# T5-bias attention with a leaky-ReLU feed-forward: another plan for the feed-forward pieces between the attention pairs

## The chip, the cores and the metric

The kernel runs on one core of one Trainium2 chip, in one launch. The metric is the device time of the whole execution in microseconds, the median of several runs; before the change it is 394.74 us (three runs, 394.33 to 396.08). A profile of one further execution goes with it. In profiles, PE is the matrix engine, PEld its weight loads, DVE the vector engine, ACT the scalar engine, POOL the general-purpose engine and SP the engine that here only issues transfers.

## The reference

```python
# q, k, v: (B=8, H=8, S=576, D=64);  bias_table: (32, 8)
scores = q @ k.T / sqrt(D) + bias_table[bucket(|i - j|)]   # per head
attn = softmax(scores)
x = (attn @ v)  ->  (B*S, H*D) = (4608, 512)
h = x @ w_in                      # 512 -> 2048
g = maximum(0.01 * h, h)
out = g @ w_out                   # 2048 -> 512
```

## The kernel before

**Pairs.** The attention is cut into 32 items, one for each batch and pair of heads: four pairs to a batch (`n_pairs` = 4), numbered n = 0 to 31 over all batches. For a pair, scores are made transposed (keys on the partitions). `qk_mm(n, u)` makes score chunk u on PE: u = 0 to 3 are 128 keys each for both heads (two banks of the pool `ps_s`, which has two such double banks), u = 4 are the last 64 queries against those keys (in the two single banks o0 and o1 of `ps_o`), u = 5 are the last 64 keys. `exp` turns each chunk into weights on ACT, `band` multiplies the chunk's diagonal band by the exponentiated bias on DVE. One pass later, `av_tails` and `av(n, 0)`, `av(n, 1)` multiply the weights with v on PE, in o0 and o1, and DVE divides by the row sums (`rcp`, `opair`, lines 383 and 384). o0 and o1 therefore go from `av` to chunk 4 of the next pair, which waits for both `opair`.

**How rows get turned.** From pair 7 on q and k are brought into place by a copy on DVE (`pair_rows`, line 268, one copy for q and one for k) and then a transposing transfer issued by SP (`turn_by_dma`, tile `tu`, line 276). `transpose_q` and `transpose_k` (lines 298 and 302) are the DVE copies that read `tu` one pass before it is needed. From pair 4 to pair 30 the attention output is turned by a transfer as well (`x_transposes`, `xT` <- `opair`, line 395); the last pair's is turned on PE and copied by DVE (lines 402 and 403). q, k and v come in through POOL's queue, batch by batch, in `loads(n)`; each group of loads begins with a tiny copy `tick` that waits for the output of pair n - 2.

**Feed-forward pieces.** The 4608 tokens are nine tiles T of 512. An *in-piece* (`ffn_in`, line 425) is four 128x512 matmuls over the four `xT` tiles, one for each pair of a batch in that order, into one bank; `leaky` then writes it to `gt`, on ACT (line 436), or on DVE in two steps (lines 433 and 434) for one piece in a block. There are 16 of them to a tile. An *out-piece* (`ffn_out`, line 450) is four matmuls as well; four of them, an *out-group*, add up in one bank, which is copied to `y` after the fourth (line 467 on DVE, or line 464 on ACT when `how["scalar"]` is set) and stored by SP. Sixteen out-pieces make a tile. All pieces during the attention take their banks in turn from `ps_m`, which has two; `moe_rest`, at the end, takes them from six places in turn (`bank`, line 409). `gt` has two buffers, so the in-pieces of a tile can begin only when the tile two before is wholly out (`can`).

**Passes.** The loop of line 700 runs passes n = 5 to 32. The order of a pass is written out by hand, and PE, DVE, ACT and SP each take their instructions in that order: `begin(n)` (loads, and `pair_rows` with `turn_by_dma` of a later pair m, three passes ahead, but two for m up to 9); chunks 0 and 1; `av_tails` and `av(n-1, 0)`; a first `slot()`; `av(n-1, 1)`; a second `slot()`; chunks 2, 3 and 4; `x_transposes(n-1)`; then `moe_block` with chunk 5 inside it. Before pass 5 the passes 0 to 4 are written out separately. The pass of n = 32 has no scores of its own; after it `moe_rest` does what is left.

`plan(n)` sets how many pieces the pass does (`groups_of`: all ready pieces but 4, spread evenly over the passes to the end of the batch, at least 4 and at most 8), and in which form. In a *lead* pass the two slots take two out-pieces each, with the copy to `y` on ACT; in any other pass a slot takes one in-piece. A batch's last `xT` counts as ready in pass 4k + 1 (`finished(n - 2)`). The rule `fresh` makes that pass a lead pass, so that the new tile's in-pieces come in the block, behind chunks 2 to 4. The pieces by pass before the change, in + out, follow from the rules:

```
pass     5   6   7   8   9  10  11  12  13  14  15  16  17  18  19  20
before  5+0 5+0 0+4 0+8 4+4 8+0 4+4 0+8 4+4 8+0 4+4 0+8 4+4 8+0 4+4 0+8
pass    21  22  23  24  25  26  27  28  29  30  31  32  rest
before  4+4 8+0 4+4 0+8 4+4 8+0 4+4 0+8 4+4 8+0 4+4 4+4 28+40
```

In the passes 9, 13, 17, ... the four out-pieces are in the slots and the four in-pieces in the block; in 11, 15, ... it is the other way round, with two of the four in-pieces in the slots.

Of the kernel before, what the change touches and what calls it, by code (L numbers as in the profile page):

```python
# [37 lines left out]
def kernel(  # L38
# [380 lines left out]
    def ffn_in(T, f):  # L419
        if f == 0:  # L420
            gts[T] = gt_pool.tile([P, n_fc, TT], BF16, name="gt")
        t0 = T * TT
        pm = bank("pm1")
        for c in range(n_cc):
            nc.tensor.matmul(pm, lhsT=w_in_sb[:, c, f * P : (f + 1) * P], rhs=xT[c][:, t0 : t0 + TT],  # L425
                             start=(c == 0), stop=(c == n_cc - 1))
        return pm

    def leaky(T, f, pm, by_vector=False):
        g = gts[T][:, f, :]  # L430
        if by_vector:
            low = low_pool.tile([P, TT], BF16, name="low")
            nc.vector.tensor_scalar(low, pm, 0.01, None, op0=ALU.mult)  # L433
            nc.vector.tensor_tensor(out=g, in0=low, in1=pm, op=ALU.max)  # L434
        else:
            nc.scalar.activation(g, pm, AF.Prelu, bias=0.0, scale=1.0, alpha=0.01)  # L436
# [41 lines left out]
    def can(kind):  # L478
        T = made[kind]
        if at_piece[kind]:  # L480
            return True
        if kind == "in":
            return T < made["ready"] and T < made["out"] + 2
        return T < made["in"]

    def step(kind):
        T, s = made[kind], at_piece[kind]
        at_piece[kind] = (s + 1) % n_fc
        if at_piece[kind] == 0:
            made[kind] += 1  # L490
        return T, s
# [22 lines left out]
    def groups_of(n):  # L514

        have = n_fc * (2 * made["ready"] - made["in"] - made["out"]) - at_piece["in"] - at_piece["out"]
        more = N + 1 if n > N - n_pairs else n - (n - 1) % n_pairs + n_pairs
        return max(4, min(8, (have - 4) // (more - n)))

    room = {"left": 0, "lead": False, "keep": 0}  # L520

    def plan(n):
        g = room["left"] = groups_of(n)
        fresh = n > n_pairs + 1 and n % n_pairs == 1
        room["lead"] = can("out") and g >= 8 and (fresh or not can("in"))
        room["keep"] = 4 if can("out") and not room["lead"] else 0

    def slot():
# [10 lines left out]
    def moe_block():  # L539

        done = 0
        if room["lead"] and can("in") or not can("out"):
            while done < 4 and room["left"] > 0 and can("in") and (room["lead"] or not can("out")):
                T, s = step("in")
                pm = ffn_in(T, s)
                leaky(T, s, pm, done == 1)
                room["left"] -= 1
                done += 1
                if done < 3:
                    yield  # L550
            if done < 1:
                yield
        if done < 3 and room["left"] >= 4 and can("out"):
            for part in range(4):
                piece_out()
                room["left"] -= 1
                if part == 1:
                    yield
        else:
            yield  # L560
        moe(2)
        yield
# [54 lines left out]
    def begin(n):  # L617
        loads(n)
        if n_pairs < n + 1 < N and not by_dma(n + 1):
            pair_rows(n + 1)  # L620
        for m in range(n + 2, min(n + AHEAD + 1, N)):
            if by_dma(m) and m - (AHEAD if m > 2 * n_pairs + 1 else 2) == n:
                pair_rows(m)
                turn_by_dma(m)

# [74 lines left out]
    for n in range(n_pairs + 1, N + 1):  # L700
        live = n < N
        more = n + 1 < N
        if x_by_dma(n - 2):
            finished(n - 2)
        plan(n)
        if live:
            begin(n)
            ps_a, ps_b = qk_mm(n, 0), qk_mm(n, 1)
            exp(n, 0, ps_a)
            exp(n, 1, ps_b)  # L710
        av_tails(n - 1)
        av(n - 1, 0)
        if live:
            band(n, 0)
        if more:
            transpose_q(n + 1)
        slot()
        av(n - 1, 1)
        if live:
            band(n, 1)  # L720
        if more:
            transpose_k(n + 1)
        slot()
        if live:
            ps_a, ps_b, ps_c = qk_mm(n, 2), qk_mm(n, 3), qk_mm(n, 4)
            exp(n, 2, ps_a)
        x_transposes(n - 1)
        while stores:
            o, y = stores.pop(0)
            nc.sync.dma_start(out=o, in_=y)  # L730
        if live:
            band(n, 2)
            exp(n, 3, ps_b)
        if not x_by_dma(n - 1):
            finished(n - 1)
        block = moe_block()
        if not can("out") or room["lead"] and can("in"):
            next(block)
        if live:
            exp(n, 4, ps_c)  # L740
        next(block)
        if live:
            band(n, 4)
            ps_a = qk_mm(n, 5)
            exp(n, 5, ps_a)
            band(n, 5)
        for _ in block:
            pass
    moe_rest()
# [30 lines left out]
```

## Time and profile before

| what | value |
|---|---|
| median of three runs | 394.74 us (394.33 to 396.08) |
| the profiled execution's own time | 395.22 us |
| its span, first to last instruction | 393.2 us |
| DVE busy | 214.4 us (55%) |
| ACT busy | 238.2 us (61%) |
| POOL busy | 76.6 us (19%) |
| mean granted clock of PE | 0.991 |
| PE matmuls of in-pieces, line 425 | 132.6 us busy |
| PE matmuls of out-pieces, line 450 | 132.4 us busy |

How to read it: an engine's busy time is the sum of its instructions' recorded durations, and a matmul's duration holds its way through the array, so back-to-back matmuls overlap in the record: they start about 0.216 us apart, while one takes about 0.38 us. A view of the span by windows gives, for each stretch, its length, then each engine's busy time with the number of its instructions, the share of the clock granted to PE, the load on the transfer engines (over 1 when requests of several queues are open at once) and the rate. A timeline row is: start, length, engine and line, the operation with its tiles, how many equal instructions are merged in the row, and in brackets the idle time before it with what ended it. A few matmul records are missing, so counts can be one or two short.

### The profile page before, as it was taken

How to read it: one execution, taken by the hardware profiler on the slowest of the kernel's cores; microseconds unless marked ns; L12 is line 12 of the kernel's file. 1: busy time of each engine (PE TensorE's matmuls, PEld its weight loads, DVE VectorE, ACT ScalarE, POOL GpSimd, SP SyncE). 2: the span in 40 equal slices, each digit the busy share in tenths (PEclk: the TensorE clock that was granted, in tenths of full speed). 3: DMA queues.
4: the chain of work that ended last, by engine and by line, in shares of the span. 5: the costliest groups of instructions: out<-in, count | busy, mean ns of one | idle time of the engine just before them, and what ended most of it. 6: DMA issues, size and time to landing. Idle time of an engine off the chain costs nothing.

```text
span 393.2 us, 8405 instructions
## 1 busy us (share of the span) xinstructions
PE 367.1 (93%) x3401; PEld 186.7 (47%) x3462; DVE 214.4 (55%) x536; ACT 238.2 (61%) x372; POOL 76.6 (19%) x118
## 2 busy tenths in 40 slices
PE   8778995999999999999999999999999998999995
PEld 3455543454455444544455445545454454444442
DVE  5698576566666656666667765675656442100221
ACT  4998784258855786568656874588358832466000
POOL 8764321221112220233022302210000000000000
PEclk9999998899999999999999999999999999999999
DMA  9999999999939981998399846992221010100122
GB/s 107 181 206 184 183 195 134 156 171 140 115 67 167 130 115 31 163 141 134 31 143 172 91 72 110 151 111 49 63 68 49 12 45 27 54 2 0 54 81 80
DMA packets 108734, 41.12 MB, mean 105 GB/s; under 512 B 87568, under 2 KB 103192, under 8 KB 108696
## 3 DMA queue, kind: packets, MB, share of 16 engines
q0 software_dynamic: 53696, 18.36, 44.6%
q1 hardware_dynamic: 54856, 22.10, 32.6%
q8 instruction: 27, 0.44, 0.5%
q10 hardware_dynamic: 144, 0.13, 0.1%
q14 instruction: 11, 0.09, 0.1%
HBM read 37.68 MB, written 9.45 MB: 120 GB/s over the span
## 4 chain that ended last, share of the span: by engine, by line
PE 64%; DVE 9%; ACT 6%; issue 3%; DVEq 0%; ACTq 0%
PE pm L450 30%; PE pm L425 20%; PE ps_o L380 8%; PE ps_s L320 5%; ACT at L333 4%; DVE opair L384 2%; ACT gt L436 2%; DVE at L356 2%; DVE kt L302 1%; DVE low L433 1%; DVE gt L434 1%; PE ps_o L369 1%; DVE qt L298 1%; DVE rcp L383 1%; PE ps_q L313 0%
## 5 line engine op out<-in xcount | busy, mean ns | idle before, releaser
L333 ACT ACTIVATE at<-ps_s 128x1024 bf16<-128x1024 f32 x128 | 124.0, 1030 | 26.1 <-PE ps_s L320 25.9
L425 PE MATMUL pm<-xT,w_in_sb 128*128 128x512 bf16 x546 | 132.6, 379 | 6.5 <-ACT gt L436 4.3
L450 PE MATMUL pm<-w_out_sb,gt 128*128 128x512 bf16 x546 | 132.4, 384 | 3.3 <-ACT gt L436 1.6
L436 ACT ACTIVATE gt<-pm 128x512 bf16<-128x512 f32 x123 | 74.1, 603 | 40.0 <-PE pm L425 39.7
L356 DVE TENSOR_TENSOR at<-at,hk 128x768 bf16<-128x768 bf16 (+3 forms) x160 | 69.8, 452 | 29.9 <-ACT at L333 19.2
L450 PEld LDWEIGHTS <-gt 128*128 128x128 bf16 x576 | 54.1, 99 | 63.1 <-issue 5.2
L425 PEld LDWEIGHTS <-w_in_sb 128*128 128x128 bf16 x576 | 52.6, 97 | 63.5 <-issue 9.3
L467 DVE COPY y<-pm 128x512 f32<-128x512 f32 x22 | 15.2, 692 | 69.3 <-PE pm L450 69.3
L380 PE MATMUL ps_o<-vn,at 128*128 128x65 bf16 x1280 | 49.4, 194 | 0.7
L380 PEld LDWEIGHTS <-at 128*128 128x128 bf16 x1280 | 44.4, 98 | 8.8 <-issue 0.7
L320 PE MATMUL ps_s<-qt,kt 64*128 64x512 bf16 x256 | 39.9, 381 | 1.7 <-ACT at L333 1.0
L383 DVE RECIPROCAL rcp<-ps_o 128x5 f32<-128x5 f32 x64 | 12.4, 194 | 48.2 <-PE ps_o L380 48.2
L464 ACT COPY y<-pm 128x512 f32<-128x512 f32 x13 | 7.6, 585 | 46.1 <-PE pm L450 46.1
L606 POOL COPY tick<-opair 1x1 bf16<-1x1 bf16 x18 | 4.6, 255 | 158.0 <-DVE opair L384 158.0
L384 DVE TENSOR_TENSOR opair<-ps_o,rcp 128x320 bf16<-128x320 f32 x64 | 31.5, 492 | 3.6 <-DVE rcp L383 0.4
L340 ACT ACTIVATE at<-ps_s 128x576 bf16<-128x576 f32 x32 | 22.4, 700 | 3.6 <-PE ps_s L324 3.6
L336 ACT ACTIVATE at<-ps_q 128x256 bf16<-128x256 f32 x64 | 22.0, 416 | 3.3 <-PE ps_q L313 3.2
L120 POOL DMA_DIRECT2D vn<-in_v_dram x24 | 21.6, 905 | 6.7 <-PE ps_s L320 2.3
L320 PEld LDWEIGHTS <-kt 64*128 64x128 bf16 x256 | 8.3, 94 | 27.2 <-issue 25.9
L433 DVE TENSOR_SCALAR low<-pm 128x512 bf16<-128x512 f32 x21 | 14.5, 691 | 9.8 <-PE pm L425 9.8
L459 ACT COPY y<-pm 128x256 f32<-128x256 f32 x1 | 0.4, 372 | 27.5 <-DVE y L458 27.5
L302 DVE COPY kt<-tu 128x576 bf16<-128x576 bf16 x25 | 17.0, 678 | 0.0
(57 smaller groups left out, 218.9 us busy)
## 6 DMA issues: line engine op xcount, KB each, us to landing
out_dram<-y SPq DMA_DIRECT2D x35, 256.0 KB, 2.8
qn<-in_q_dram POOLq DMA_DIRECT2D x14, 288.0 KB, 6.2
kn<-in_k_dram POOLq DMA_DIRECT2D x14, 288.0 KB, 7.3
vn<-in_v_dram POOLq DMA_DIRECT2D x28, 128.0 KB, 7.3
w_in_sb<-in_moe_w_in_dram POOLq DMA_DIRECT2D x2, 1024.0 KB, 12.9
w_out_sb<-in_moe_w_out_dram POOLq DMA_DIRECT2D x2, 1024.0 KB, 18.0
qn<-in_q_dram POOLq DMA_DIRECT2D x4, 144.0 KB, 3.9
kn<-in_k_dram POOLq DMA_DIRECT2D x4, 144.0 KB, 4.1
```

Of the source, the lines that this page charges most:

```text
L120: nc.gpsimd.dma_start(out=vn[i][:, c, :, 0:D], in_=v[b, :, c * P : (c + 1) * P, :].rearrange("h s d -> s h d"),)
L302: nc.vector.tensor_copy(out=kt[:, 0:S].rearrange("p (r c) -> p r c", c=NC), in_=turned_pair(n, 1))
L320: nc.tensor.matmul(ps[:, e, :], lhsT=kt[r, u * P : (u + 1) * P], rhs=qt[r, 0:512], start=True, stop=True)
L333: nc.scalar.activation(at[:, :, u, 0:512], ps, AF.Exp, scale=scale)
L336: nc.scalar.activation(at[:, e, :, 512:S], ps[e][:, 0 : NJ * SL].rearrange("p (c i) -> p c i", i=SL), AF.Exp, scale=scale)
L340: nc.scalar.activation(at4[:, 0:S], ps.rearrange("p e i -> p (e i)")[:, 0:S], AF.Exp, scale=scale)
L356: nc.vector.tensor_tensor(out=o, in0=o, in1=m, op=ALU.mult)
L380: nc.tensor.matmul(ps[:, ic, :], lhsT=at[:, o : o + P], rhs=vn[b % NBUF][:, c, 2 * p + e, :], start=False, stop=(ic == NJ and c == NJ - 1))
L384: nc.vector.tensor_tensor(out=opair[:, :, e * D : (e + 1) * D], in0=ps[:, :, 0:D], in1=rcp.to_broadcast([P, NJ + 1, D]), op=ALU.mult)
L425: nc.tensor.matmul(pm, lhsT=w_in_sb[:, c, f * P : (f + 1) * P], rhs=xT[c][:, t0 : t0 + TT], start=(c == 0), stop=(c == n_cc - 1))
L436: nc.scalar.activation(g, pm, AF.Prelu, bias=0.0, scale=1.0, alpha=0.01)
L450: nc.tensor.matmul(pm, lhsT=gt[:, f, ts * P : (ts + 1) * P], rhs=w_out_sb[:, f, :], start=(f == 0), stop=(f == n_fc - 1))
```

## The change

```diff
@@ groups_of
-        return max(4, min(8, (have - 4) // (more - n)))
+        keep = min(n_fc, 4 * ((n - 1) // n_pairs)) if more <= N else 0
+        return max(4, min(8, (have - keep) // (more - n)))
@@ plan
-        fresh = n > n_pairs + 1 and n % n_pairs == 1
-        room["lead"] = can("out") and g >= 8 and (fresh or not can("in"))
+        room["lead"] = can("out") and g >= 8 and not can("in")
@@ moe_block
-        if room["lead"] and can("in") or not can("out"):
-            while done < 4 and room["left"] > 0 and can("in") and (room["lead"] or not can("out")):
-                T, s = step("in")
-                pm = ffn_in(T, s)
-                leaky(T, s, pm, done == 1)
-                room["left"] -= 1
-                done += 1
-                if done < 3:
-                    yield
-            if done < 1:
+        while not can("out") and can("in") and done < 4 and room["left"] > 0:
+            T, f = step("in")
+            leaky(T, f, ffn_in(T, f), done == 1)
+            room["left"] -= 1
+            done += 1
+            if done < 3:
                 yield
-        if done < 3 and room["left"] >= 4 and can("out"):
+        while done < 2:
+            done += 1
+            yield
+        if can("out") and room["left"] >= 4:
@@ begin
-            if by_dma(m) and m - (AHEAD if m > 2 * n_pairs + 1 else 2) == n:
+            if by_dma(m) and m - (AHEAD if m > 2 * n_pairs + 2 else 2) == n:
@@ the passes from 5 on
-        if live:
-            band(n, 2)
-            exp(n, 3, ps_b)
-        if not x_by_dma(n - 1):
+        if not live:
             finished(n - 1)
+            break
+        band(n, 2)
         block = moe_block()
-        if not can("out") or room["lead"] and can("in"):
+        next(block)
+        exp(n, 3, ps_b)
+        next(block)
+        exp(n, 4, ps_c)
+        if can("out"):
             next(block)
-        if live:
-            exp(n, 4, ps_c)
-        next(block)
-        if live:
-            band(n, 4)
-            ps_a = qk_mm(n, 5)
-            exp(n, 5, ps_a)
-            band(n, 5)
+        band(n, 4)
+        ps_a = qk_mm(n, 5)
+        exp(n, 5, ps_a)
+        band(n, 5)
         for _ in block:
             pass
```

What it does: the number of pieces that `groups_of` holds back grows by 4 with each batch up to 16, in place of a constant 4. A pass is a lead pass only when no in-piece can be done. So from pass 21 on every pass has the same shape: one in-piece in each slot, one whole out-group around chunk 5 in the block, and two in-pieces after it. In a block without out-pieces the first in-piece and its `leaky` now stand before `exp` of chunk 3. The rows of pair 10 are copied and turned in pass 8, next to those of pair 11, and no longer in pass 7. In pass 32 nothing follows the last pair's turn, so the pieces after it belong to `moe_rest` with its six places. By the rules:

```
pass     5   6   7   8   9  10  11  12  13  14  15  16  17  18  19  20
after   5+0 5+0 0+4 0+8 3+4 7+0 6+0 0+8 3+4 3+4 7+0 3+4 3+4 3+4 3+4 7+0
pass    21  22  23  24  25  26  27  28  29  30  31  32  rest
after   4+4 4+4 4+4 4+4 4+4 4+4 4+4 4+4 4+4 4+4 4+4 2+0 34+52
```

The pieces are the same 144 + 144 in all. The pieces whose `leaky` runs on DVE go from 21 to 6, the full copies to `y` on ACT (line 464) from 13 to 2. In the passes 9, 13, 17, 21, 25 and 29 the new tile's first in-piece stands in the first slot, directly behind `av(n-1, 0)`.

## The prediction

> **What bounds the kernel now.** I read the page first: busy shares, the slices, the chain of waits.
>
> ```profile
> span 393.2 us, 8405 instructions
> ...
> PE 367.1 (93%) x3401; PEld 186.7 (47%) x3462; DVE 214.4 (55%) x536; ACT 238.2 (61%) x372; POOL 76.6 (19%) x118
> ...
> DMA  9999999999939981998399846992221010100122
> ...
> PE 64%; DVE 9%; ACT 6%; issue 3%; DVEq 0%; ACTq 0%
> ```
>
> PE is busy for 93% of the span and makes up 64% of the chain that ended last; no other engine reaches 10% of it. The transfer engines are full for eleven slices of 9.8 us, then with a nearly idle slice in every four. So two questions matter: where PE still waits, and whether an early wait is really one for transfers.
>
> Next the view by windows, cut where `av_tails` starts on PE: the passes 7, 9, 21, 22, 23 and 24, then all from pass 32 on.
>
> ```profile
> 58.97:73.19 14.22, 9.67 (x85) 4.55 (x84) 6.58 (x19) 5.35 (x9) 1.50 (x3) 0.76 1.74 138
> 83.12:93.61 10.49, 10.11 (x100) 5.14 (x100) 7.73 (x19) 6.88 (x11) 2.86 (x4) 1.00 1.58 189
> ...
> 206.93:217.41 10.48, 10.10 (x100) 5.12 (x100) 7.71 (x19) 6.87 (x11) 2.87 (x4) 1.00 1.06 152
> 217.41:227.89 10.48, 9.98 (x100) 5.13 (x100) 6.47 (x16) 8.72 (x15) 3.11 (x5) 1.00 1.01 120
> 227.89:238.24 10.35, 9.97 (x100) 5.13 (x100) 6.29 (x15) 6.61 (x12) 0.00 (x0) 1.00 0.17 34
> 238.24:248.17 9.93, 9.82 (x100) 5.07 (x100) 6.04 (x16) 5.46 (x9) 2.62 (x4) 1.00 1.16 144
> ...
> 320.30:393.20 72.90, 67.50 (x353) 31.39 (x359) 10.55 (x18) 19.46 (x33) 0.00 (x0) 1.00 0.12 44
> ```
>
> The passes 21 to 24 hold eight pieces each and the same attention work, but take 10.48, 10.48, 10.35 and 9.93 us. The shortest has only out-pieces; the others lose 0.55, 0.55 and 0.42 us. From pass 9 to 31 the pattern repeats every four passes. The timeline of PE shows the loss, in pass 22 and then in pass 24:
>
> ```profile
> 218.28 0.81 PE L425 MATMUL pm<-xT,w_in_sb 128*128 128x512 bf16 x3
> ...
> 223.31 0.19 PE L324 MATMUL ps_s<-qt,kt 128*128 128x64 bf16 x1
> 223.78 0.81 PE L425 MATMUL pm<-xT,w_in_sb 128*128 128x512 bf16 x3 [0.27 <-ACT gt L436]
> 224.76 2.75 PE L425 MATMUL pm<-xT,w_in_sb 128*128 128x512 bf16 x12 [0.18 <-DVE gt L434]
> ...
> 245.88 0.19 PE L324 MATMUL ps_s<-qt,kt 128*128 128x64 bf16 x1
> 245.91 1.89 PE L450 MATMUL pm<-w_out_sb,gt 128*128 128x512 bf16 x8
> ```
>
> After the last matmul of chunk 5 the next piece starts 0.03 us later in pass 24, 0.47 us later in pass 22: it waits for a bank of `ps_m` that `leaky` on ACT still reads, and one piece on for the bank that DVE reads (0.11 us beyond four matmuls of 0.216). Up to chunk 5 nothing is lost: 223.31 is 5.90 us behind the pass's start with four pieces done, 245.88 is 7.64 with six, and two pieces are 1.73. So an in-piece in a slot costs PE only its matmuls; two or more in the block cost a wait.
>
> **Part by part: the passes 21 to 31.** Before, six of them lose 0.55 and three 0.42: 4.56 us. After, all are alike, with two in-pieces in the slots, an out-group around chunk 5 and two in-pieces behind. ACT is not in the way: it is busy for 8.72 us in the pass of in-pieces alone and 5.46 in the one of out-pieces, and a half-and-half pass lies between, below 9.93. The one new wait is the last in-piece's: it takes the bank of the out-group, with one in-piece between.
>
> ```profile
> 237.80 0.61 PE L320 MATMUL ps_s<-qt,kt 64*128 64x512 bf16 x4
> ...
> 237.90 0.69 DVE L467 COPY y<-pm 128x512 f32<-128x512 f32 x1 [2.15 <-PE pm L450]
> ```
>
> In pass 23 the out-group ends where the next chunk starts, at 237.80, and the copy to `y` at 238.59, 0.79 us later. The in-piece between covers 0.87, less the passing of the semaphore, so I take 0.1 us; the bounds are 0 and 0.7 (a copy wholly uncovered). Eleven times 0.1 is 1.1: **a gain of 3.5 us**, between a loss of 3.1 and a gain of 4.6.
>
> **The passes 9 to 20, banks alone.** Before: three times 1.52, 4.56 us. After: passes 12 and 8 are unchanged lead passes, seven have an out-group in the block and lose nothing (three in-pieces, so none behind a fresh out-group's bank), and four have in-pieces alone (10, 11, 15, 20) and keep a loss of 0.55, since the piece on DVE still holds its bank as long: 2.2. Moving the first `leaky` ahead of chunk 3's `exp` only shifts which of the two banks is late. **Gain 2.4 us**; bounds 0 (every moved wait comes back) and 4.6. The twelve pieces fewer before pass 32 and more behind it cost the same on PE at either place: 0.
>
> **The rows of pair 10.** The 14.22 us of pass 7, with only four pieces and the clock at 0.76, are the longest loss. PE, DVE and the transfer of pair 8's rows:
>
> ```profile
> 61.05 0.61 PE L320 MATMUL ps_s<-qt,kt 64*128 64x512 bf16 x4
> 64.33 0.20 PE L313 MATMUL ps_q<-qt,kt 64*128 64x64 bf16 x1 [2.67 <-DVE opair L384]
> 65.85 0.39 PE L313 MATMUL ps_q<-qt,kt 64*128 64x64 bf16 x7 [1.31 <-DVE opair L384]
> ...
> 63.23 0.36 DVE L268 COPY pr<-kn 96x768 bf16<-96x768 bf16 x1 [1.21 <-DMA kn<-in_k_dram]
> ...
> 64.53 0.64 DVE L298 COPY qt<-tu 128x576 bf16<-128x576 bf16 x1
> ...
> 65.30 0.49 DVE L384 TENSOR_TENSOR opair<-ps_o,rcp 128x320 bf16<-128x320 f32 x1
> ...
> L276 SPq DMA_TRANSPOSE tu<-pr x1: 1717/1717/1717, 53.1 to 53.1; - x1
> DMA to landing us min/median/max: 10.9/10.9/10.9
> ```
>
> Chunk 4 waits for `opair`, which DVE does late because pair 10's second copy waited for k until 63.23. Taking that copy away seems to free over 3 us. But DVE's next hold stands right behind it: the copy `qt` of line 298 reads pair 8's `tu`, issued at 53.1 and landed 10.9 us later, at 64.04. `qt` ran at 64.53, so everything from there moves by **0.5 us**; that landing hangs on transfers issued before the change acts. In pass 8, DVE takes pair 10's and pair 11's copies together; `av` there has two out-pieces behind it, so this hides. The bounds of the gain are 0 and the whole wait, 65.85 less 61.5, 4.4 us, if that landing did not bind.
>
> **The first in-piece of a tile.** In pass 9 the piece moves from behind chunk 4 into the first slot. Its fourth matmul needs the `xT` of pair 7. The issues on SP, the piece on PE, and three transfers of `xT` with their landings:
>
> ```profile
> 74.11 2.03 SPq L276 DMA_TRANSPOSE tu<-pr  x1
> 77.36 2.19 SPq L395 DMA_TRANSPOSE xT<-opair  x1
> ...
> 88.81 1.90 PE L425 MATMUL pm<-xT,w_in_sb 128*128 128x512 bf16 x7
> ...
> L395 SPq DMA_TRANSPOSE xT<-opair x1: 2192/2192/2192, 77.4 to 77.4; - x1
> DMA to landing us min/median/max: 9.7/9.7/9.7
> ...
> L395 SPq DMA_TRANSPOSE xT<-opair x1: 2131/2131/2131, 67.6 to 67.6; - x1
> DMA to landing us min/median/max: 12.2/12.2/12.2
> ...
> L395 SPq DMA_TRANSPOSE xT<-opair x1: 1364/1364/1364, 118.7 to 118.7; - x1
> DMA to landing us min/median/max: 6.8/6.8/6.8
> ```
>
> Before, `xT` landed at 77.4 + 9.7 = 87.1 and the piece began at 88.81: no wait. After, pass 9 starts at 83.12 - 0.5 = 82.6; the slot comes 0.87 us later (218.28 less 217.41), its fourth matmul 0.65 after that: 84.1. SP now issues two `tu` ahead of this `xT` (74.11 - 0.5 = 73.6, 2.03 each), so `xT` goes out at 77.7, not 76.9. Landing takes 6.8 us at least (the transfer issued at 118.7, in a thinner stretch) and 12.2 at most (issued at 67.6, right behind a `tu`). Its own row says 9.7, the one behind a `tu` 12.2, and it is now behind two; I take the middle, 11: 88.7, and PE waits from 84.1: **a loss of 4.6 us**, bounds 0.4 (landed at 84.5) and 5.8 (at 89.9). Queued behind it on PE are `av(8, 1)` and the chunks 2 to 5 of pair 9, so ACT and DVE idle too; no cover is left.
>
> At the later batch starts (13, 17, 21, 25) the same matmul is due 9.93 + 0.87 + 0.65 = 11.45 us after the start of the pass before, and `xT` is issued 4.17 after it (77.36 less 73.19): 7.3 us for landing, where 6.8 was seen. A shorter pass before it takes up to 0.9 off. I put 0.1 at each: **a loss of 0.4 us**, bounds 0 and a rival's price below.
>
> **The end.** PE from pass 32 on:
>
> ```profile
> 326.08 2.75 PE L425 MATMUL pm<-xT,w_in_sb 128*128 128x512 bf16 x12 [0.39 <-ACT y L464]
> 329.51 1.02 PE L425 MATMUL pm<-xT,w_in_sb 128*128 128x512 bf16 x4 [0.69 <-ACT gt L436]
> ...
> 361.45 27.79 PE L450 MATMUL pm<-w_out_sb,gt 128*128 128x512 bf16 x125
> ```
>
> The last pair's turn has nothing behind it, and PE idles 0.39 us; three in-pieces then wait for the two banks, 329.51 less (326.08 + 2.59) = 0.84, and 0.2 more before line 450 goes on. After, an out-group and two in-pieces, 5.2 us, cover the turn's copy, and `moe_rest` has six places. The four-matmul pieces there run at 27.8 us for 128 matmuls either way. I leave 0.1 for the shorter cover ahead of the turn: **gain 1.3 us**, bounds 0.5 and 1.5.
>
> **The sum**, against the profiled execution's 395.22: -0.5 + 4.6 + 0.4 - 2.4 - 3.5 - 1.3 = -2.7, so 392.5. The median lies 0.48 below that execution: **392.0 us**, 0.7% faster.
>
> **The rivals.**
>
> *The clock drops in pass 9.* A wait of 4.6 us is as long as the one of pass 7 (from 61.5 to 65.85, with one short matmul in it), and there the clock fell:
>
> ```profile
> 65.80:67.00 1.20, 0.93 (x9) 0.52 (x10) 1.17 (x4) 0.66 (x2) 0.00 (x0) 0.50 2.06 119
> ```
>
> It was granted at 0.50 behind that wait, and 0.76 over the 14.22 us is 3.4 us of clock lost, some 0.5 of it before PE had work: 2.9 us. Then 394.9. For it: the like length. Against it: most of the range of the wait is shorter. The Trainium skill (TensorE: Matmul & The Clock Gate, Part 1) says that one idle window of about 3.4 us halves the clock, and that the windows run free of the program; the row agrees that a wait beyond that length can do it, and by the rule a wait of 4.6 us need not fill a window.
>
> *No wait in pass 9.* With pair 10's rows gone from pass 7, the transfers have less ahead of them, and `xT` lands in 6.8 us, with a wait of 0.4 left: 387.8. Against it: the same transfers are only issued later, directly ahead of this one.
>
> *Slower: the batch starts wait on transfers every time.* Before, the rule `fresh` kept 5 us between a landing and its first reader. If the denser passes make `xT` land in 9.7 us at the passes 13, 17, 21 and 25, each waits 9.7 - 7.3 = 2.4 us: 392.0 - 0.4 + 9.6 = 401.2. It decides from a landing time of 7.3 us on. For it: 6.8 is only half a microsecond away, and a store of `y` now goes out ahead in nearly every pass. Against it: from slice 12 on the transfer engines have a slack slice in each batch, so loads no longer pile up from one to the next.
>
> *The change doesn't do what it says* holds for pair 10's rows, and is in the sum.
>
> **How the numbers follow.** A measurement of this kernel can tell about 0.5% from no change, 2.0 us: faster is below 392.8, slower above 396.7. The forecast has 0.45, with a range of its own of 389 to 394 (the wait of pass 9 and the copy to `y` between their bounds), two thirds of it faster: 0.30 faster, 0.15 same. The clock's drop has 0.20: 0.17 same, 0.03 slower. No wait has 0.17, faster. Waits at every batch have 0.18: 0.16 slower, 0.02 same. Together 0.47, 0.34 and 0.19. The range of 387.0 to 398.0 takes in the first two, nearly all of the third and leaves most of the fourth out.
>
> **What would show it.** In the profile after: passes 21 to 31 at 10.0 us each, with a short idle before the last in-piece that ends with DVE's `y`; pass 7 at 13.7 us, with chunk 4 still late and `qt` waiting for `tu`; in pass 9 an idle of line 425 that ends with a transfer of `xT`, and behind it the granted clock, 1.0 or 0.5; no waits around 326 us before the end's run. Wrong would make it: an idle before line 425 in every pass 4k + 1, passes with four and four pieces above 10.4 us, or pass 7 shorter by 3 us.

## The result, and the profile after

The changed kernel takes **393.35 us** (median of 13 runs, 388.46 to 399.91) against 396.08 us for the kernel before on the same chip (13 runs, 394.18 to 400.43): a ratio of 0.989, interval 0.985 to 0.993, so 1.1% faster. The ratio, like those below, sets only the runs within 1.5% of each kernel's fastest against each other (here 8 against 11); by the medians of all runs the change is 0.7%. Ten further runs of it gave 0.990 (0.985 to 0.994). Its first profiled execution, 396.43 us, was longer than that median, so a second one of 390.33 us is read beside it; the two differ most in pass 9.

The page of the first profile, as far as it answers to the lines shown of before:

```profile
span 394.6 us, 8469 instructions
...
PEclk9999999977999999999999999999999999999999
...
PE 81%; DMA 10%; DVE 5%; ACT 2%; issue 1%; POOL 0%; POOLq 0%
```

PE is still the bound. New are the 10% of the chain that is now a wait for transfers (half of it for loads of k, a quarter each for `xT` and `tu`, by the page's next row), and two slices (78.9 to 98.6 us) with the clock granted at 0.7. The view by windows says where the time went. First the first profile (passes 7, 9, 20 and 21, and everything from pass 32 on), then the second (passes 7 and 9, the passes 10 to 31 as one window, and the rest; pass 8 takes 9.93 us in all three):

```profile
59.05:68.66 9.61, 6.84 (x87) 3.66 (x85) 5.54 (x16) 5.27 (x9) 1.35 (x2) 1.00 1.80 128
...
78.59:99.31 20.72, 10.67 (x98) 5.35 (x96) 6.99 (x18) 6.38 (x10) 2.88 (x4) 0.75 1.47 121
191.59:201.22 9.63, 9.24 (x100) 4.68 (x97) 6.57 (x17) 8.13 (x14) 2.99 (x4) 1.00 1.19 152
201.22:211.23 10.01, 10.01 (x102) 5.07 (x100) 6.18 (x15) 7.04 (x12) 2.88 (x4) 1.00 1.46 108
...
310.82:394.60 83.78, 78.03 (x408) 35.99 (x407) 10.56 (x18) 22.46 (x38) 0.00 (x0) 1.00 0.12 44
```

```profile
60.70:72.01 11.31, 8.25 (x85) 4.06 (x84) 5.54 (x16) 5.26 (x9) 1.47 (x2) 0.85 1.81 138
...
81.94:92.19 10.25, 9.18 (x98) 4.68 (x96) 6.92 (x18) 6.39 (x10) 2.87 (x4) 1.00 1.39 171
92.19:304.29 212.10, 208.19 (x2118) 107.01 (x2151) 130.50 (x324) 153.46 (x240) 37.82 (x55) 1.00 0.75 102
304.29:388.50 84.21, 77.45 (x400) 35.99 (x407) 10.56 (x18) 22.46 (x38) 0.00 (x0) 0.99 0.12 44
```

Set against the windows of before, where the passes 10 to 31 take 320.30 - 93.61 = 226.69 us, and with each piece that moved (12 more from pass 32 on) priced at 27.8 / 32 = 0.87 us, the sum of the prediction reads, in us:

```
                                        predicted   first profile   second profile
start of pass 7                             0            0.1             1.7
pass 7                                     -0.5         -4.6            -2.9
pass 9, piece counted (wait 4.6 - 0.55)    +4.1        +11.1            +0.6
passes 10 to 31 (-1.85 - 3.5 + 0.4)        -5.0         -5.6            -5.0
from pass 32 to the last matmul            -1.3         -1.3            -1.5
behind the last matmul                      0           +1.8            +2.4
span against before (393.2)                -2.7         +1.4            -4.7
```

Here "passes 10 to 31" is -15.2 and -14.6 us as measured, less the eleven pieces gone from them (9.55). Pass 7 began between 58.8 and 60.7 us in the profiles of this kernel and its variants; none of that is put down to the change. The dense part came out as forecast. PE's waits for `leaky`, summed before and then after (us in total, times, longest):

```profile
PE pm L425 <- ACT gt L436: 4.3, 15, 0.7
...
PE pm L450 <- ACT gt L436: 1.6, 6, 0.3
```

```profile
PE pm L425 <- DVE gt L434: 1.6, 4, 0.4
...
PE pm L425 <- ACT gt L436: 0.2, 1, 0.2
```

The waits for ACT are gone but for 0.2 us; those for DVE's piece go from 1.1 us before to 1.6. A pass with four and four pieces takes 10.01 us (10.03 predicted), and its last in-piece's wait for the bank is the 0.07 us by which the first of these rows exceeds a pair of pieces without a wait (1.90); the second shows pass 32 going through its turn without an idle:

```profile
218.89 1.97 PE L425 MATMUL pm<-xT,w_in_sb 128*128 128x512 bf16 x8
...
314.44 3.62 PE L450 MATMUL pm<-w_out_sb,gt 128*128 128x512 bf16 x16
317.90 15.70 PE L425 MATMUL pm<-xT,w_in_sb 128*128 128x512 bf16 x72
```

The four passes with in-pieces alone keep their wait for DVE's piece, 0.4 each (the first row of after). Pass 20 takes 9.63 us for its seven pieces, where pass 14 of the second profile, with an out-group in its block, takes 9.06: 0.57 more.

**Pass 9.** First PE and SP of the first profile, then of the second, and for each the two issues of `tu` on SP (count, shortest, middle and longest in ns) and the landing of that `xT`:

```profile
79.45 0.81 PE L425 MATMUL pm<-xT,w_in_sb 128*128 128x512 bf16 x3
90.32 0.59 PE L425 MATMUL pm<-xT,w_in_sb 128*128 128x512 bf16 x1 [10.05 <-DMA xT<-opair]
...
79.98 2.38 SPq L395 DMA_TRANSPOSE xT<-opair  x1
...
L276 SPq DMA_TRANSPOSE tu<-pr x2: 3961/5110/6258, 69.6 to 73.6; - x2
...
DMA to landing us min/median/max: 10.3/10.3/10.3
```

```profile
84.64 0.38 PE L425 MATMUL pm<-xT,w_in_sb 128*128 128x512 bf16 x1 [1.01 <-DMA xT<-opair]
...
77.89 1.34 SPq L395 DMA_TRANSPOSE xT<-opair  x1
...
L276 SPq DMA_TRANSPOSE tu<-pr x2: 1339/2392/3445, 72.9 to 74.4; - x2
...
DMA to landing us min/median/max: 6.7/6.7/6.7
```

The reader is the same matmul in both, the fourth of that in-piece, but it is due at 80.1 us in one (79.45 + 3 x 0.216) and at 83.5 in the other. The two `tu` ahead of `xT` take SP 10.2 or 4.8 us, `xT` then lands after 10.3 or 6.7 us, and PE waits 10.05 or 1.01 us. The two kernels of *The end* below have the same passes 7 to 9; in their profiles `xT` landed after 6.0 and 6.9 us, and PE waited 1.3 and 1.9.

**Pass 7.** DVE's `qt` and PE's chunk 4 and first out-piece, in the first profile and then PE in the second:

```profile
62.86 0.64 DVE L298 COPY qt<-tu 128x576 bf16<-128x576 bf16 x1 [1.63 <-DMA tu<-pr]
...
64.19 0.29 PE L313 MATMUL ps_q<-qt,kt 64*128 64x64 bf16 x7 [2.63 <-DVE opair L384]
64.41 1.90 PE L450 MATMUL pm<-w_out_sb,gt 128*128 128x512 bf16 x8
```

```profile
65.91 0.31 PE L313 MATMUL ps_q<-qt,kt 64*128 64x64 bf16 x7 [2.70 <-DVE opair L384]
...
66.97 2.69 PE L450 MATMUL pm<-w_out_sb,gt 128*128 128x512 bf16 x6 [0.22 <-issue]
```

Chunk 4 still waits for `opair`, and `opair` behind `qt` for the landing of `tu`. In the first profile `qt` ran at 62.86 in place of 64.53 and PE's clock did not fall (eight matmuls in 1.90 us); in the second six matmuls take 2.69 us, the half clock. Five more profiles have the same pass 7 (pair 7 on PE, `tu` behind `xT`, pass 9 as a lead pass, and the two of *The end*): it takes 9.6, 10.9, 11.3, 11.6, 11.9, 13.3 and 13.5 us in the seven. Most of that spread is the clock. Its share over the window gives the time at half clock as length x (1 - share) / 0.5: none in the first profile, 3.3 to 3.5 us in the next four, 6.7 to 6.9 in the last two, as in pass 7 of before (14.22 x 0.24 / 0.5 = 6.8).

**The end.** The last matmuls on PE and ACT's issue of the last store, before, after (first profile), and the page's row on the fetching of ACT's instructions in both (packets, MB, share):

```profile
379.80 9.44 PE L450 MATMUL pm<-w_out_sb,gt 128*128 128x512 bf16 x42
...
390.14 0.37 ACTq L461 DMA_DIRECT2D out_dram<-y  x1
...
q14 instruction: 11, 0.09, 0.1%
```

```profile
379.62 9.23 PE L450 MATMUL pm<-w_out_sb,gt 128*128 128x512 bf16 x42
...
389.75 2.13 ACTq L461 DMA_DIRECT2D out_dram<-y  x1
...
q14 instruction: 12, 0.10, 0.1%
```

Before, the span ends 4.0 us behind the last matmul (393.2 - 389.24), after it 5.75 us (394.6 - 388.85), 6.4 in the second profile. ACT's issue takes 2.13 us in place of 0.37 (2.59 in the second profile), and one more block of instructions was fetched. That q14 is ACT's queue is inferred: its count changes when ACT's program does, while the other instruction queue, q8, shows 27 in every profile.

### The profile page after: what moved, and what is told of

Same layout as the page of the kernel before. It is cut to its first block, busy times and chain, and to the rows that moved or that the text cites. A ratio compares the mean times of both kernels' runs of the same rounds, so it can differ in the third digit from the quotient of the medians.

```text
span 394.6 us, 8469 instructions
## 1 busy us (share of the span) xinstructions
PE 365.7 (93%) x3462; PEld 184.4 (47%) x3462; DVE 203.5 (52%) x517; ACT 240.3 (61%) x376; POOL 76.7 (19%) x118
## 4 chain that ended last, share of the span: by engine, by line
PE 81%; DMA 10%; DVE 5%; ACT 2%; issue 1%; POOL 0%; POOLq 0%
PE pm L450 32%; PE pm L425 28%; PE ps_o L380 9%; PE ps_s L320 7%; DMA kn<-in_k_dram 5%; DMA xT<-opair 3%; DMA tu<-pr 3%; ACT at L333 1%; PE ps_o L369 1%; PE ps_s L323 1%; DVE opair L384 1%; PE ps_q L313 1%; DVE at L356 1%; DVE low L433 1%; DVE gt L434 1%
## 5 line engine op out<-in xcount | busy, mean ns | idle before, releaser
L425 PE MATMUL pm<-xT,w_in_sb 128*128 128x512 bf16 x576 | 140.7, 381 | 11.9 <-DMA xT<-opair 10.1
L436 ACT ACTIVATE gt<-pm 128x512 bf16<-128x512 f32 x138 | 83.0, 602 | 101.0 <-PE pm L425 100.4
L356 DVE TENSOR_TENSOR at<-at,hk 128x768 bf16<-128x768 bf16 (+3 forms) x160 | 71.4, 453 | 33.7 <-ACT at L336 18.9
L450 PEld LDWEIGHTS <-gt 128*128 128x128 bf16 x576 | 53.0, 98 | 60.6
L467 DVE COPY y<-pm 128x512 f32<-128x512 f32 x33 | 22.8, 692 | 76.5 <-PE pm L450 76.5
L380 PEld LDWEIGHTS <-at 128*128 128x128 bf16 x1280 | 44.9, 98 | 19.1 <-issue 11.3
L120 POOL DMA_DIRECT2D vn<-in_v_dram x24 | 22.9, 959 | 7.1 <-PE ps_s L324 3.7
L298 DVE COPY qt<-tu 128x576 bf16<-128x576 bf16 x25 | 16.3, 651 | 7.0 <-DMA tu<-pr 7.0
L112 POOL DMA_DIRECT2D qn<-in_q_dram x18 | 13.8, 768 | 3.7 <-DMA qn<-in_q_dram 1.5
```

The source lines that it names most:

```text
L120: nc.gpsimd.dma_start(out=vn[i][:, c, :, 0:D], in_=v[b, :, c * P : (c + 1) * P, :].rearrange("h s d -> s h d"),)
L356: nc.vector.tensor_tensor(out=o, in0=o, in1=m, op=ALU.mult)
L380: nc.tensor.matmul(ps[:, ic, :], lhsT=at[:, o : o + P], rhs=vn[b % NBUF][:, c, 2 * p + e, :], start=False, stop=(ic == NJ and c == NJ - 1))
L450: nc.tensor.matmul(pm, lhsT=gt[:, f, ts * P : (ts + 1) * P], rhs=w_out_sb[:, f, :], start=(f == 0), stop=(f == n_fc - 1))
L467: nc.vector.tensor_copy(out=y, in_=pm)
```

## The experiments

Two theories on the early passes. The *late-transfer theory*: the wait of pass 9 is one of order; `xT` of pair 7 stands on SP's queue behind two `tu`, and its reader has come forward from the block to the first slot, so that either another place for the issue or another place for the reader removes it. The *backlog theory*: the loads of the first 90 us bound these passes, and what is won at one landing is lost at the next. On the end, the *fetch theory*: ACT's instructions have grown until a new block begins right at the last store. Ratios below are to the kernel before on the same chip, with their intervals.

**The changed kernel again.** No edit.

> The changed kernel once more, as the partner of the other three. First theory (late transfer): PE waits 8 to 10 us before line 425 in pass 9 for the xT of pair 7, which SP issues only after two tu transfers whose issue took 10.3 us in the profiled run; time 0.989 of before. Rival (backlog): the same wait, but it is the sum of all transfers up to some 90 us that ends it, not the place of any one. Both expect the same here: pass 7 near 9.6 us, pass 10 starting at 96 to 99 us.

Measured: 392.49 us (389.69 to 397.05), 0.990 (0.985 to 0.994). Its profile is the second one above.

**The wait of pass 9 taken away in three ways.** Pair 7's output turned on PE in place of SP:

```diff
-        return n_pairs <= n < N - 1
+        return n_pairs <= n < N - 1 and n != 2 * n_pairs - 1
...
-        if x_by_dma(n - 2):
+        if n - 2 >= n_pairs:
```

> The output of pair 7 alone is turned on PE and copied by DVE, as the last pair's is, in place of a transfer. Late transfer: no wait for xT in pass 9; what is left is pair 10's tu, which holds qt on DVE until about 85 us and so chunk 4 until 86.5; pass 10 starts at 91 to 92 us in place of 99.3, and the time falls by 6 to 8 us against the changed kernel, to 0.970 to 0.975 of before. Backlog: the wait goes to tu and to the loads of k instead, pass 10 starts at 96 or later, and the time falls by less than 3 us.

Measured: 389.43 us, 0.981 (0.973 to 0.989). Pair 11's `tu` issued behind that `xT`, no longer ahead of it:

```diff
-                turn_by_dma(m)
+                if m != 2 * n_pairs + 3:
+                    turn_by_dma(m)
...
         x_transposes(n - 1)
+        if n == 2 * n_pairs:
+            turn_by_dma(n + AHEAD)
```

> Only the place on SP's queue changes: the turn of pair 11's rows is issued behind the xT of pair 7 in pass 8 and no longer ahead of it. Late transfer: xT goes out near 74 us and lands at 82 to 85, the wait in pass 9 falls to 2 to 5 us, the time by 5 to 7 us against the changed kernel, to 0.971 to 0.976 of before. Backlog: xT still lands at 88 or later and the time falls by less than 2 us.

Measured: 388.65 us (387.11 to 389.65), 0.979 (0.971 to 0.987). And the reader put back into the block, in pass 9 alone, as the rule `fresh` had it:

```diff
-        room["lead"] = can("out") and g >= 8 and not can("in")
+        fresh = n == 2 * n_pairs + 1
+        room["lead"] = can("out") and (fresh or g >= 8 and not can("in"))
```

> Pass 9 alone is made a lead pass as before the change: the out-group in the slots, the new tile's three in-pieces in the block. Late transfer: the xT of pair 7 lands where it did, at 84 to 90 us, but its first reader comes some 5 us later in the pass, so the wait for it shrinks by up to 5 us and the bank waits of the block (0.4 to 0.6 us) come back; pass 9 takes 9.5 to 10 us where the landing is early, 12 to 15 where it is late; time 0.981 to 0.986 of before, with less spread than the changed kernel. Backlog: pass 9's length does not depend on where the piece stands, time 0.988 to 0.992.

Measured: 387.24 us (387.09 to 387.57), 0.973 (0.965 to 0.981). The window of pass 9 with pair 7 on PE, SP's issue of `xT` and PE's first in-piece with the other order, and PE in pass 9 with the lead pass:

```profile
81.01:90.08 9.07, 8.97 (x98) 4.68 (x97) 7.05 (x18) 6.39 (x10) 2.87 (x4) 1.00 1.57 194
```

```profile
74.78 1.43 SPq L395 DMA_TRANSPOSE xT<-opair  x1
...
81.42 1.19 PE L425 MATMUL pm<-xT,w_in_sb 128*128 128x512 bf16 x4
```

```profile
87.72 1.90 PE L425 MATMUL pm<-xT,w_in_sb 128*128 128x512 bf16 x8
```

With `xT` issued at 74.78 in place of 77.9 to 80.0, the in-piece of pass 9 runs through (four matmuls in 1.19 us); with its reader at 87.72 in place of 79.5 to 82.8, nothing waits either, though `xT` goes out as late as 77.2. The wait goes when either place is changed, as the late-transfer theory has it; the backlog's signs (pass 10 at 96 or later, `xT` landed at 88 or later) did not come. The three ratios lie 0.9 to 1.7 hundredths below that of the changed kernel, the last with its whole interval below 0.985, the lower end of that kernel's; the other two intervals overlap it. The first two gain less than was expected (0.970 to 0.976), the third more (0.981 to 0.986): the expectations reckoned with the wait of the first profile, which three of the four profiles with the same passes 7 to 9 do not have. With the lead pass `xT` landed at 84.5 (77.2 + 7.3), so in that profile the reader in the slot, due at 83.55, would have waited only 1 us. About 2 us of that last one's gain come from the end, not from pass 9: there ACT's last issue takes 0.38 us and the span ends 4.1 us behind the last matmul (below); in the other two it takes 2.4 us, between the 2.13 and 2.59 of the changed kernel. All 16 runs of these three kernels and the next one lie between 385.8 and 390.9 us; the 23 of the changed kernel between 388.5 and 399.9.

**The same for all four pairs of that batch.** The outputs of the pairs 4 to 7 turned on PE, so that no `xT` stands ahead of pair 8's `tu` either:

```diff
-        return n_pairs <= n < N - 1
+        return 2 * n_pairs <= n < N - 1
...
-        if x_by_dma(n - 2):
+        if n - 2 >= n_pairs:
```

> The outputs of the pairs 4 to 7 are turned on PE and copied by DVE, so that four transposing transfers fewer stand on SP's queue in passes 5 to 8. Late transfer: the tu of pair 8 is no longer behind two xT and lands at 58 to 61 us, qt in pass 7 does not wait for it, pass 7 takes 7.5 to 8.5 us without a clock drop, and pass 9 waits for no xT; what is left is the load of k for pair 12, 0 to 3 us on DVE in pass 9; time 0.965 to 0.974 of before. Backlog: tu and the loads land no earlier, pass 10 starts at 90 or later, time above 0.978.

Measured: 388.5 us (385.82 to 390.88), 0.976 (0.964 to 0.987). The `qt` of pass 7 on DVE:

```profile
63.65 0.65 DVE L298 COPY qt<-tu 128x576 bf16<-128x576 bf16 x1 [0.98 <-DMA tu<-pr]
```

The expected earlier `tu` did not come: `qt` still waits for it until 63.65, where the profiles of the other kernels have 62.9 to 65.3. The chain of waits shows why: the load of pair 8's k ends at 53.2 after 17.2 us, `tu` goes out at 53.58 (51.7 to 54.1 in the others) and lands after 10.05 us, with no `xT` about. That landing does not hang on SP's order; here the backlog theory holds (pass 10 begins at 90.66; the ratio lies between the two expectations).

**Pair 10's rows.** The move undone in the changed kernel (the diff), and the move alone made in the kernel before (its reverse):

```diff
-            if by_dma(m) and m - (AHEAD if m > 2 * n_pairs + 2 else 2) == n:
+            if by_dma(m) and m - (AHEAD if m > 2 * n_pairs + 1 else 2) == n:
```

> Only the move of pair 10's rows is undone. Late transfer: pass 7 is back at 13 to 14.5 us with DVE held by the load of k until 63, the xT of pair 7 goes out behind one tu and lands near 87, so the wait in pass 9 shrinks to about 2.5 us; pass 10 starts at 94 to 95, 4 us earlier than the changed kernel, time 0.978 to 0.98 of before. Backlog: what pass 7 loses pass 9 gains, pass 10 starts within 1.5 us of the changed kernel's, time 0.985 to 0.993.

> The kernel before, with only the move of pair 10's rows to pass 8. If the move gains by itself: pass 7 falls from 14.2 to 9.6 to 11.5 us, and since the first in-piece of the new tile stands in the block of pass 9 the later xT costs 0 to 2 us there; time 0.990 to 0.994 of before. If it gains nothing (the prediction's sum gave it 0.5 us): 0.998 to 1.002, pass 7 at 13.5 us or longer, or the gain of pass 7 lost again in pass 9.

Measured: undone, 394.92 us (391.67 to 399.77), 0.987 (0.976 to 0.999); made alone, 394.41 us (10 runs), 0.995 (0.990 to 0.999). Undone, DVE and PE in pass 7; made alone, the same two:

```profile
63.59 0.36 DVE L268 COPY pr<-kn 96x768 bf16<-96x768 bf16 x1 [2.80 <-DMA kn<-in_k_dram]
...
66.20 0.39 PE L313 MATMUL ps_q<-qt,kt 64*128 64x64 bf16 x7 [1.31 <-DVE opair L384]
```

```profile
64.55 0.64 DVE L298 COPY qt<-tu 128x576 bf16<-128x576 bf16 x1 [2.55 <-DMA tu<-pr]
...
65.88 0.39 PE L313 MATMUL ps_q<-qt,kt 64*128 64x64 bf16 x7 [3.85 <-DVE opair L384]
```

Without the move DVE waits for k until 63.59, with it for `tu` until 64.55, and chunk 4 comes at 66.20 or 65.88. The next hold stands right behind the first, as the prediction said. Made alone, pass 7 takes 13.76 us in place of 14.22, close to the 0.5 of the prediction, and pass 10 begins 0.1 us earlier in that profile; the ratio gives about half a per cent, and no profile shows where more than 0.5 us would come from. Undone, only one `tu` stands ahead of `xT`, which goes out at 77.68, and PE still waits 1.70 us in pass 9, so the second `tu` is not needed for a wait.

**Pass 7 shortened on purpose.** Pass 7 as a lead pass, its out-pieces in the slots ahead of chunk 4; then the passes 7 and 9 both; then both with pair 11's `tu` behind `xT` of pair 7 as above:

```diff
-        room["lead"] = can("out") and g >= 8 and not can("in")
+        fresh = n == 2 * n_pairs - 1
+        room["lead"] = can("out") and (fresh or g >= 8 and not can("in"))
```

```diff
-        fresh = n == 2 * n_pairs - 1
+        fresh = n == 2 * n_pairs - 1 or n == 2 * n_pairs + 1
```

> Pass 7 alone is made a lead pass: its four out-pieces stand in the slots, ahead of the chunk 4 that waits for DVE, and no longer behind it. Late transfer, with pass 9 as in the changed kernel: PE has 3.5 us of work before the wait, so pass 7 has little idle time and no clock drop and takes 6.5 to 8 us in place of 9.6 to 13.5; but pass 9 then comes to the xT of pair 7 all the earlier, whose landing stays at 84 to 90 us, and waits 6 to 13 us; pass 10 starts at 92 to 99, the time stays at 0.982 to 0.990 of before. Rival (pass 7's wait and half clock are a loss of their own): pass 10 starts 4 to 6 us earlier, time 0.970 to 0.976.

> Passes 7 and 9 are lead passes; SP's order is the changed kernel's. Late transfer: pass 7 as in the run before, but the xT of pair 7 goes out behind two tu and lands at 82 to 89, so pass 9 waits 0 to 6 us in its block; pass 10 starts at 87 to 93, time 0.962 to 0.975 of before, with more spread than the run before. Backlog: the same as the run before within 1 us.

> Passes 7 and 9 are lead passes, and the turn of pair 11's rows is issued behind the xT of pair 7. Late transfer: pass 7 at 6.5 to 8 us without a clock drop, the xT of pair 7 out near 70 us and landed at 78 to 83, its first reader at 82 or later; pass 10 starts at 85 to 89 us, time 0.958 to 0.968 of before. Backlog: the loads and tu end pass 9 at 90 or later whatever PE does, time 0.970 to 0.976.

Measured: 394.96 us (10 runs), 0.990 (0.986 to 0.995); 391.16 us, 0.986 (0.976 to 0.995); 387.12 us (385.57 to 392.60), 0.971 (0.963 to 0.979). PE with pass 7 as a lead pass, and SP's two `tu`; PE in pass 9 with both; DVE and PE in pass 9 with the order changed as well:

```profile
65.54 0.29 PE L313 MATMUL ps_q<-qt,kt 64*128 64x64 bf16 x7 [0.33 <-DVE opair L384]
...
89.47 0.58 PE L425 MATMUL pm<-xT,w_in_sb 128*128 128x512 bf16 x1 [7.92 <-DMA xT<-opair]
...
L276 SPq DMA_TRANSPOSE tu<-pr x2: 4117/5034/5951, 69.1 to 73.3; - x2
```

```profile
89.34 2.29 PE L425 MATMUL pm<-xT,w_in_sb 128*128 128x512 bf16 x5 [3.42 <-DMA xT<-opair]
```

```profile
83.43 0.73 DVE L298 COPY qt<-tu 128x576 bf16<-128x576 bf16 x1 [2.58 <-DMA tu<-pr]
...
86.95 1.24 PE L425 MATMUL pm<-xT,w_in_sb 128*128 128x512 bf16 x5 [1.07 <-DMA xT<-opair]
```

The wait ahead of chunk 4 falls to 0.33 us, and the time of the whole does not move: the reader of `xT` comes earlier, SP's `tu` take 4.1 and 6.0 us, and 7.92 us are waited in pass 9, within the 6 to 13 that the late-transfer theory expected. With pass 9 a lead pass too, 3.42 us remain, and the time misses what either theory gave; with the order changed, 1.07, and then `qt` waits for a `tu` until 83.43. There pass 10 begins at 90.24 and the ratio is 0.971, which is what the backlog theory expected (90 or later, 0.970 to 0.976), not the late-transfer theory. In the four profiles without a long wait in pass 9 that have pair 7 on PE or the later `tu`, pass 10 begins at 89.8 to 90.7 us. So both theories have a part: the order decides who waits in pass 9, the landings how much there is to win before it. Whether another order of the loads would let pass 10 begin earlier was not tried.

**The end.** The last half store issued by SP in place of ACT, and three small copies at the kernel's start moved from ACT to DVE, so that ACT has three instructions fewer:

```diff
-            nc.scalar.dma_start(out=o[:, h:DM], in_=y[:, h:DM])
+            nc.sync.dma_start(out=o[:, h:DM], in_=y[:, h:DM])
```

```diff
-        copy = nc.scalar.copy if j % 3 == 2 else nc.vector.tensor_copy
-        copy(out=ub[:, C0 + lo : C0 + lo + m * w].rearrange("h (m w) -> h m w", w=w),
+        nc.vector.tensor_copy(out=ub[:, C0 + lo : C0 + lo + m * w].rearrange("h (m w) -> h m w", w=w),
```

> The last half row block's store is issued by SP in place of ACT; nothing else. In five profiles of kernels with the new plan that issue on ACT took 2.1 to 2.6 us, before 0.37, and the end came 6.1 to 6.3 us behind the last matmul in place of 4.1; their ACT queue shows a twelfth fetch of instructions, before eleven. Fetch theory: the issue waits for that block of instructions, so from SP it takes 0.4 us and the end comes 4.0 to 4.6 us behind the last matmul; time 2 us below the changed kernel, near 0.984 to 0.986 of before. Rival (the store itself is slow at the end): the end stays 6 us behind.

> Three small copies that build the bias row, at the start of the program, go from ACT to DVE; nothing else changes. Fetch theory: ACT's program is three instructions shorter, the twelfth fetch of its instructions goes away or moves off the last issue, that issue takes 0.4 us and the end comes 4.1 us behind the last matmul in place of 6.2; time 2 us below the changed kernel, near 0.984 of before. Rival (the last store is slow by itself): 6 us behind, time as the changed kernel.

Measured: 391.5 us (388.81 to 398.79), 0.982 (0.962 to 1.002), and 391.47 us (389.07 to 396.27), 0.981 (0.973 to 0.990). The last matmuls, the last issue (line 460 there) and the fetches with three instructions fewer on ACT:

```profile
379.78 4.91 PE L449 MATMUL pm<-w_out_sb,gt 128*128 128x512 bf16 x22
...
385.59 0.37 ACTq L460 DMA_DIRECT2D out_dram<-y  x1
...
q14 instruction: 11, 0.09, 0.1%
```

The issue is back at 0.37 us, the twelfth fetch is gone, and the span ends 4.1 us behind the last matmul (388.8 - 384.69) in place of 5.75 and 6.4. With the store on SP the twelfth fetch stays, the issue takes 0.38 us there, and the end is 4.7 us behind. (The expectation's 6.1 to 6.3 us for the end is 5.75 to 6.4 by the profiles.) Set side by side, the fourteen profiles read:

```
ACT busy instructions   372  373  376  377  376              376
fetches on q14           11   11   11   12  12, once 13       12, store on SP
profiles                  2    1    1    3   6                 1
last issue, us         0.37 0.37 0.38 0.37  2.13 to 2.59      0.38
```

The count of busy instructions alone does not tell where a block begins, since issues and semaphores are not in it. A store that is slow by itself is ruled out, since from SP its issue takes 0.38 us and the end comes sooner; that a fetch falls right into ACT's issue is inferred from these counts, as no view times the fetch. The profiles agree with the fetch theory; the medians of these two, which still have pass 9's wait, are too widely spread to price it.

## Why the prediction was right

The forecast was 392.0 us, 0.7% faster, and the median came out at 393.35 us, 2.7 us below that of the kernel before on the same chip; the ratio gives 1.1%. The dense passes came out by their mechanism. That the whole came so near is in part luck: pass 7 gained more than forecast, pass 9 lost less in three of four profiles and far more in one, and the end lost what the forecast did not have; these partly cancel. Point by point:

- **Passes 10 to 31: right, in mechanism and size.** -5.6 and -5.0 us against -5.0; passes of 10.01 us against 10.03; the all-in passes kept a loss of 0.57 (0.55 predicted), 0.4 of it the wait, the copy to `y` cost 0.07 (0.1). The 0.4 us for the later batch starts was no more than that: the second profile has such waits of 1.4 us in all, 1.0 of it in pass 9.
- **Up to the last matmul: right,** -1.3 and -1.5 against -1.3.
- **The wait for `xT` in pass 9: right in place and cause, mis-sized.** The forecast was 4.6 us, and four profiles of that pass show 1.0, 1.3, 1.9 and 10.05. Two steps were off. "I take the middle, 11" for the landing: it was 6.0, 6.7, 6.9 and 10.3. In the second profile `xT` went out at 77.89, as forecast (77.7), and the short landing alone made the short wait. And "pass 9 starts at 83.12 - 0.5 = 82.6" held the reader fixed: in the first profile pass 9 starts at 78.59, 4.0 us earlier, while `xT` landed at 90.3, only 1.6 later than the forecast's 88.7; the two are the excess. There the step "SP now issues two `tu` ahead of this `xT` (74.11 - 0.5 = 73.6, 2.03 each), so `xT` goes out at 77.7" was off as well, by 2.3 us. A transposing issue has no fixed length in this stretch. In the ten profiles that have both `tu` next to each other, ahead of or without that `xT`, the start of the first and the time that SP spent on the two were (us):

```
start  69.1  69.6  70.1  71.7  72.3  72.9  73.0  73.4  74.0  74.0
both   10.1  10.2   8.2   5.8   3.4   4.8   4.0   5.5   5.8   4.1
```

  The three that went out before 71 us took the longest; that they then stand deeper in the loads is a reading of this table, not shown by itself. The longest issues go with the earliest reader, and the prediction had bounded each apart from the other, so the wait could pass its bound of 5.8. (Its own range of 389 to 394 is also narrower than those bounds: 0.4 to 5.8 for the wait and 0 to 0.7 for eleven copies give 386.7 to 399.8.)
- **Pass 7: right in the order of the holds, mis-sized.** The prediction gave 0.5 us since `qt` waits for `tu`, and `qt` did; in seven profiles pass 7 lost 0.8 to 4.6 us, and the prediction's own sign of being wrong, "pass 7 shorter by 3 us", came in the first. The landing moved (`qt` ran between 62.9 and 65.3), and the clock behind the wait decided more than the wait. In the first profile chunk 4 came 65.85 - 64.19 = 1.7 us earlier, and the other 2.9 us of its 4.6 is the half clock that stayed away, the price that the prediction had worked out for it. That a gain there brings SP's `tu` deeper into the loads and the reader of `xT` forward, and so is paid back in pass 9, was not in the sum; pass 7 as a lead pass shows it.
- **The end behind the last matmul: put at nothing, without a reason;** it was +1.8 and +2.4 us.

Of the rivals, *the clock drops in pass 9* did happen in the first profile. The granted clock behind the wait, and later:

```profile
90.30:92.00 1.70, 1.68 (x22) 1.36 (x22) 0.00 (x0) 0.60 (x1) 0.00 (x0) 0.50 1.49 197
92.00:94.20 2.20, 2.20 (x17) 0.67 (x15) 1.93 (x5) 0.55 (x2) 0.00 (x0) 0.68 1.73 157
```

It cost about 1.6 us (20.72 less 9.06 and the wait of 10.05), not the 2.9 of pass 7, since it was back some 3 us behind the wait. *No wait* (0.4 us) is nearer to three of the four profiles (1.0 to 1.9) than the forecast's 4.6. *Waits at every batch start* did not come: the passes 13 to 29 of the two profiles show at most 0.4 us. *The change doesn't do what it says* fits pair 10's rows, whose next hold stood ready.

In sum, the change is worth some 6.5 us of denser passes and end, gives about 2 of it back at the last store, wins 0.8 to 4.6 in pass 7 and loses 0.6 to 11 in pass 9. The kernel with pass 9 alone as a lead pass, 387.24 us, beats the changed kernel by about 1.7% and the one before by 2.7%, by the ratios, and stayed within 0.5 us in four runs; the one with both lead passes and the later `tu` has a median of 387.12 us but a run at 392.6.

## What to carry to other kernels

When the first reader of a transferred tile moves forward, look at what stands ahead of its issue on the issuing engine, and price the wait as a range from the shortest and longest issues and landings of that stretch, and move its reader along, not from one row. Where transfers are backed up, a pass that becomes shorter brings the next reader to its landing earlier, so a gain there counts only after the next wait has been looked up. And look at the last instruction of every engine behind the last matmul: an issue that is suddenly 2 us long may come from the fetching of instructions.

## What the runs showed of the hardware

A transposing transfer's issue on SP took 1.3 us in a thin stretch and up to 6.3 us among loads, within the same program from run to run.

ACT's last issue took 2.13 to 2.59 us in the six profiles with 376 busy instructions on ACT and twelve or thirteen fetches of some 8 KB (0.10 MB in 12 packets), and 0.37 us both with three instructions fewer (373, eleven fetches) and with one more (377, twelve fetches). That a fetch right at the issue holds it is inferred from this. The Trainium skill (Runtime: NRT & Kernel Launch, Instruction fetch mechanics) says that crossing a block of instructions is mostly hidden; if the slow issue is such a crossing, some 2 us of this one are not.

The half clock came in stretches of about 3.4 us or whole multiples of it, worked out as above from length and clock share. In pass 7 there was none or one stretch behind idles of PE of 2.2 to 3.6 us (six profiles), and two, 6.7 to 6.9 us, behind idles of 3.8 to 4.1 (three profiles, and two with 4.0 to 4.1 in two parts). In pass 9 of the first profile it began during the idle of 10.05 us, at about 83.2, and ended some 3 us behind it, at about 93.4: 10.2 us. In pass 9 of the kernel with three instructions fewer on ACT an idle of 1.94 us was enough for one stretch (12.75 x 0.13 / 0.5 = 3.3). So the length of an idle alone does not tell whether the clock falls. The Trainium skill (TensorE: Matmul & The Clock Gate, Part 1) gives a busy window of about 3.4 us for the clock's return: the single stretches agree, and the longer ones are as long as two and three such windows.
